# A decode block's weight and cache loads: one ring of 16 KiB slots on one queue, longer weight runs, accumulation by contraction chunk, and a last product in four column groups

## The chip, the cores and the metric

The kernel runs on one core of a Trainium2 chip. The metric is the device time of one execution in microseconds (us). Each kernel was timed in several rounds together with the kernel before on the same chip. The profile comes from one such execution; its span, from the first instruction to the last, is 1.7 to 2.0 us shorter than the reported time.

Engine names: PE is the TensorE's matmul side and PEld its weight loads; DVE is the VectorE, ACT the ScalarE, POOL the GpSimd, SP the SyncE. A "q" after the name means that engine's instruction queue, for example SPq, from which the loads are issued. HBM is the memory that holds the tensors, and SBUF the on-chip memory of 128 partitions in which loads land. L95 is line 95 of that kernel's source.

## The reference, cut to what matters

A decoder block for 4 sequences with one new token each: layer norm, attention over a cached window, and a gated feed-forward part. All tensors are bf16.

```python
# x (4,1,1024); k_cache, v_cache (4 batch, 4 kv heads, 8192, 128)
# wq (1024,4096)  wo (4096,1024)  w1, w3 (1024,3584)  w2 (3584,1024)
def _A_ref(x, k_cache, v_cache, wq, wo):
    W = min(4096, max(256, Sk // 4))            # 2048: the last 2048 keys
    q = (x @ wq).reshape(B, Sq, 32, 128).transpose(0, 2, 1, 3)
    k = jnp.repeat(k_cache[:, :, Sk - W:, :], 8, axis=1)
    v = jnp.repeat(v_cache[:, :, Sk - W:, :], 8, axis=1)
    p = softmax(einsum("bhqd,bhkd->bhqk", q, k) * 128 ** -0.5)
    return einsum("bhqk,bhkd->bhqd", p, v).transpose(...).reshape(B, Sq, 4096) @ wo
def _B_ref(x, w1, w3, w2):
    return (silu(x @ w1) * (x @ w3)) @ w2
h  = x + _A_ref(layernorm(x), k_cache, v_cache, wq, wo)
h2 = h + _B_ref(layernorm(h), w1, w3, w2)
```

With 4 rows of activations nearly every byte is used once: 55.6 MB of weights and cache must come from HBM (8.4 MB each for wq, K, V and wo; 7.3 MB each for w1, w3 and w2). The arithmetic is small.

## The kernel before

The parts that matter here, with cuts marked by "...". The SBUF tiles that receive the stream come from three pools. A padding tile in front of them moves their start to a multiple of 4096 bytes in each partition:

```python
    wq_v = A_wq.rearrange("(kc p) n -> p kc n", p=P)
    wo_v = A_wo.rearrange("(h p) n -> p h n", p=P)
    w1_v = B_w1.rearrange("(kc p) f -> p kc f", p=P)
    ...
    first_base = -(-nc.sbuf_base // 32) * 32
    pad_bytes = (-first_base) % 4096
    if pad_bytes:
        padpool = ctx.enter_context(tc.tile_pool(name="padpool", bufs=1))
        pad_t = padpool.tile([P, pad_bytes], mybir.dt.uint8)
    wpool = ctx.enter_context(tc.tile_pool(name="wpool", bufs=4))
    kpool = ctx.enter_context(tc.tile_pool(name="kpool", bufs=4))
    vpool = ctx.enter_context(tc.tile_pool(name="vpool", bufs=2))
```

Each load is one DMA of 2 MB. wq, w1 and w3 are read in blocks of 1024 output columns, so each contiguous piece (a "run") has 1024 x 2 bytes = 2 KiB; the last blocks of w1 and w3 have 512 columns, 1 KiB. K and V have runs of 4 KiB, wo and w2 of 2 KiB. V is issued from another queue (GpSimd).

```python
        dma.dma_start(out=wq_t[:], in_=wq_v[:, :, hb * HB * P : (hb + 1) * HB * P])     # dma = nc.sync
    ...
        nc.gpsimd.dma_start(out=vbig[:],
            in_=A_v_cache[b0, g0 : g0 + BGT, Sk - W : Sk, :].rearrange("g (p j) d -> p g j d", j=NK))
    ...
    FBLOCKS = [8, 8, 8, 4]
        dma.dma_start(out=w_t[:, :, : FB * P], in_=w_v[:, :, fc0_ * P : (fc0_ + FB) * P])
    ...
        dma.dma_start(out=w2_t[:, :FCB, :], in_=w2_v[:, fc0 : fc0 + FCB, :])
```

The last product uses 4 of the 128 output partitions, and its last load is 1 MB:

```python
    y2_ps = psB2.tile([B, D], FP32, tag="y2")
    ...
            for n in range(2):
                nc.tensor.matmul(y2_ps[:, n * 512 : (n + 1) * 512],
                    lhsT=hgT[:, fc, :], rhs=w2_t[:, fs, n * 512 : (n + 1) * 512],
                    start=(fc == 0), stop=(fc == FC - 1))
    res = act.tile([B, D], BF16)
    nc.vector.tensor_tensor(out=res[:], in0=y2_ps[:], in1=h1bd[:], op=ALU.add)
    dma.dma_start(out=out_flat, in_=res[:])
```

Of the kernel before, what the change touches and what calls it, by code (L numbers as in the profile page):

```python
# [10 lines left out]
P = 128  # L12
ACT = mybir.ActivationFunctionType
ALU = mybir.AluOpType
AX = mybir.AxisListType
BF16 = mybir.dt.bfloat16
FP32 = mybir.dt.float32

DEBUG = False
# [3 lines left out]
def kernel(  # L23
# [26 lines left out]
    assert Dh == P and W == NK * P and B * Hq == P  # L50
# [5 lines left out]
    wq_v = A_wq.rearrange("(kc p) n -> p kc n", p=P)  # L56
    wo_v = A_wo.rearrange("(h p) n -> p h n", p=P)
    w1_v = B_w1.rearrange("(kc p) f -> p kc f", p=P)
    w3_v = B_w3.rearrange("(kc p) f -> p kc f", p=P)
    w2_v = B_w2.rearrange("(fc p) n -> p fc n", p=P)  # L60

    dma = nc.sync

    if DEBUG:
        dbg_pool = ctx.enter_context(tc.tile_pool(name="dbg", bufs=1, space=bass.MemoryType.DRAM))

    def dump(name: str, ap: bass.AP):
        if not DEBUG:
            return
        t = dbg_pool.tile(list(ap.shape), ap.dtype, name=name, uniquify=False)  # L70
        nc.sync.dma_start(out=t[:], in_=ap)

    first_base = -(-nc.sbuf_base // 32) * 32
    pad_bytes = (-first_base) % 4096
    if pad_bytes:
        padpool = ctx.enter_context(tc.tile_pool(name="padpool", bufs=1))
        pad_t = padpool.tile([P, pad_bytes], mybir.dt.uint8)
    wpool = ctx.enter_context(tc.tile_pool(name="wpool", bufs=4))
    kpool = ctx.enter_context(tc.tile_pool(name="kpool", bufs=4))
    vpool = ctx.enter_context(tc.tile_pool(name="vpool", bufs=2))  # L80
# [3 lines left out]

    ident = const.tile([P, P], BF16)
    make_identity(nc, ident[:])
    eps_t = const.tile([P, 1], FP32)
    nc.vector.memset(eps_t[:], eps)

    WQB = 5  # L90
    HB = 8
    wq_tiles = []
    for hb in range(Hq // HB):
        wq_t = wpool.tile([P, KC, HB * P], BF16, tag="w16k")
        dma.dma_start(out=wq_t[:], in_=wq_v[:, :, hb * HB * P : (hb + 1) * HB * P])  # L95
        wq_tiles.append(wq_t)
        if hb == 0:
            x_sb = act.tile([B, D], BF16)
            dma.dma_start(out=x_sb[:], in_=x_flat)

    def layernorm_bf16(x_in_ap: bass.AP, tag: str) -> bass.AP:
        stats = act.tile([B, 2, nc.vector.BN_STATS_DIM], FP32, tag=tag + "_stats")
        for c in range(2):
            nc.vector.bn_stats(out=stats[:, c, :], in_=x_in_ap[:, c * 512 : (c + 1) * 512])
        mv = act.tile([B, nc.vector.BN_AGGR_DIM], FP32, tag=tag + "_mv")
        nc.vector.bn_aggr(out=mv[:], in_=stats[:])
        rstd = act.tile([B, 1], FP32, tag=tag + "_rstd")
        nc.scalar.activation(
            out=rstd[:], in_=mv[:, 1:2], func=ACT.Sqrt, bias=eps_t[:B], scale=1.0
        )  # L110
        nc.vector.reciprocal(out=rstd[:], in_=rstd[:])
        xn = act.tile([B, D], BF16, tag=tag + "_xn")
        nc.vector.tensor_scalar(  # L113
            out=xn[:],
            in0=x_in_ap,
            scalar1=mv[:, 0:1],
            scalar2=rstd[:, 0:1],
            op0=ALU.subtract,
            op1=ALU.mult,
        )  # L120
        return xn

    def transpose_bd_to_db(psum_pool, xn_ap: bass.AP, tag: str) -> bass.AP:
        tp_ps = psum_pool.tile([P, KC, B], BF16, tag="kt0")
        for kc in range(KC):
            nc.tensor.transpose(  # L126
                out=tp_ps[:, kc, :],
                in_=xn_ap[:, kc * P : (kc + 1) * P],
                identity=ident[:B, :B],
            )  # L130
        xT = act.tile([P, KC, B], BF16, tag=tag + "_xT")
        nc.vector.tensor_copy(out=xT[:], in_=tp_ps[:])
        return xT
# [3 lines left out]

    xn = layernorm_bf16(x_sb[:], "ln1")
    xnT = transpose_bd_to_db(psA, xn[:], "ln1")
    dump("dbg_xn", xn[:])  # L140
    dump("dbg_xnT", xnT[:])

    qT_ps = psA.tile([P, Hq, B], FP32, tag="kt1")
    for hb in range(Hq // HB):
        wq_t = wq_tiles[hb]
        for hh in range(HB):
            h = hb * HB + hh
            for kc in range(KC):
                nc.tensor.matmul(  # L149
                    qT_ps[:, h, :],  # L150
                    lhsT=wq_t[:, kc, hh * P : (hh + 1) * P],
                    rhs=xnT[:, kc, :],
                    start=(kc == 0),
                    stop=(kc == KC - 1),
                )

    Qm = act.tile([P, B * Hkv, P], BF16)
    nc.vector.memset(Qm[:], 0.0)
# [9 lines left out]
    dump("dbg_Qm", Qm[:])  # L168
# [3 lines left out]
    BGT = 4  # L172
    kbig_tiles = []
    for bt in range(B * Hkv // BGT):
        kbig = kpool.tile([P, BGT, NK, Dh], BF16, tag="kslot")
        b0, g0 = divmod(bt * BGT, Hkv)
        dma.dma_start(  # L177
            out=kbig[:],
            in_=A_k_cache[b0, g0 : g0 + BGT, Sk - W : Sk, :].rearrange("g (p j) d -> p g j d", j=NK),
        )  # L180
        kbig_tiles.append(kbig)
    for bg in range(B * Hkv):
        b, g = divmod(bg, Hkv)
        k_t = kbig_tiles[bg // BGT][:, bg % BGT]
        kT = ktpool.tile([P, NK, P], BF16, tag="kT")
        JPB = 4
        for jb in range(NK // JPB):
            kt_ps = psA.tile([P, JPB, P], FP32, tag=f"kt{jb % 4}")
            for jj in range(JPB):
                j = jb * JPB + jj  # L190
                nc.tensor.matmul(kt_ps[:, jj, :], lhsT=k_t[:, j, :], rhs=ident[:], start=True, stop=True)  # L191
            if jb % 2 == 0:
                nc.vector.tensor_copy(out=kT[:, jb * JPB : (jb + 1) * JPB, :], in_=kt_ps[:])  # L193
            else:
                nc.scalar.copy(out=kT[:, jb * JPB : (jb + 1) * JPB, :], in_=kt_ps[:])  # L195
        kT_tiles.append(kT)

        def emit_scores(bg2):
            for n in range(NSB):
                nc.tensor.matmul(  # L200
                    scores_ps[:, n * 512 : (n + 1) * 512],
                    lhsT=Qm[:, bg2, :],
                    rhs=kT_tiles[bg2][:, n * 4 : (n + 1) * 4, :],
                    start=(bg2 == 0),
                    stop=(bg2 == B * Hkv - 1),
                )

        if bg >= 1:
            emit_scores(bg - 1)
    emit_scores(B * Hkv - 1)  # L210

    v_tiles = []
    for bt in range(B * Hkv // BGT):
        b0, g0 = divmod(bt * BGT, Hkv)
        if bt < 2:
            vbig = vpool.tile([P, BGT, NK, Dh], BF16, tag="vslot")
        else:
            vbig = kpool.tile([P, BGT, NK, Dh], BF16, tag="kslot")
        nc.gpsimd.tensor_copy(out=vbig[0:1, 0, 0, 0:1], in_=Qm[0:1, 0, 0:1])
        nc.gpsimd.dma_start(  # L220
            out=vbig[:],
            in_=A_v_cache[b0, g0 : g0 + BGT, Sk - W : Sk, :].rearrange("g (p j) d -> p g j d", j=NK),
        )
        for gg in range(BGT):
            v_tiles.append(vbig[:, gg])
# [8 lines left out]
        out=Pm[:], in_=scores_ps[:], func=ACT.Exp, bias=nmax[:], scale=1.0,  # L234
        accum_out=rsum[:],
# [4 lines left out]
    nc.vector.tensor_scalar(  # L240
        out=Dm[:], in0=ident[:], scalar1=rinv[:, 0:1], scalar2=None, op0=ALU.mult
    )
    dump("dbg_Pm", Pm[:])
    dump("dbg_rsum", rsum[:])

    PT_sb = act.tile([P, NK, P], BF16)
    JB = 4
    for jb in range(NK // JB):
        pt_ps = psA.tile([P, JB, P], FP32, tag=f"kt{jb % 4}")
        for jj in range(JB):  # L250
            j = jb * JB + jj
            nc.tensor.matmul(  # L252
                pt_ps[:, jj, :],
                lhsT=Pm[:, j * P : (j + 1) * P],
                rhs=Dm[:],
                start=True,
                stop=True,
            )
        nc.vector.tensor_copy(out=PT_sb[:, jb * JB : (jb + 1) * JB, :], in_=pt_ps[:])  # L259
    dump("dbg_PT", PT_sb[:])  # L260

    OT_ps = psA.tile([P, B, Hq], FP32, tag="kt1")
    for bg in range(B * Hkv):
        b, g = divmod(bg, Hkv)
        v_t = v_tiles[bg]
        for j in range(NK):
            nc.tensor.matmul(  # L267
                OT_ps[:, b, g * REP : (g + 1) * REP],
                lhsT=v_t[:, j, :],
# [3 lines left out]
            )  # L273
    OT_sb = act.tile([P, Hq, B], BF16)
    nc.vector.tensor_copy(out=OT_sb[:].rearrange("p h b -> p b h"), in_=OT_ps[:])
    dump("dbg_OT", OT_sb[:])
    psA_cm.__exit__(None, None, None)

    psB_cm = tc.tile_pool(name="psB", bufs=1, space=bass.MemoryType.PSUM)
    psB = psB_cm.__enter__()  # L280
    xT = transpose_bd_to_db(psB, x_sb[:], "x")
    dump("dbg_hnT0", xT[:])
    yT_ps = psB.tile([P, KC, B], FP32, tag="yt")
    HB2 = 8
    wo_tiles = []
    for hb in range(Hq // HB2):
        wo_t = wpool.tile([P, HB2, D], BF16, tag="w16k")
# [154 lines left out]
```

## Time and profile before

| | before |
|---|---|
| time, median of 4 runs (lowest to highest) | 149.81 us (149.66 to 151.16) |
| span of the profile | 147.8 us |
| PE busy, DVE busy | 59%, 25% |
| moved by DMA | 55.8 MB in 24,542 packets |

Three lines of the profile's page cut the span into 40 equal slices of 3.7 us. DMA is the busy share of the 16 DMA engines in tenths (9 is 90% or more), GB/s what they moved, and the third line sums the packets. One data packet is one contiguous run; the packet records of the trace have 17,928 of 2 KiB, 4,096 of 4 KiB and 2,048 of 1 KiB, and the 456 packets under 512 B are records of 4 bytes.

```profile
DMA  4999999999999999999999999999999999999600
GB/s 96 408 410 409 406 406 423 422 413 421 422 419 419 420 421 412 419 414 408 409 406 407 405 411 402 404 409 404 408 405 408 386 387 401 409 410 408 247 6 2
DMA packets 24542, 55.81 MB, mean 378 GB/s; under 512 B 456, under 2 KB 2504, under 8 KB 24528
```

The DMA engines are full from the second slice to the 37th, while no other engine is full throughout. So the kernel is bound by its stream of loads, and only two things count: how fast the stream runs, and what comes after its end. The windows view gives the rate in chosen stretches. Its columns are the stretch in us and its length, then busy us (and instructions) of PE, PEld, DVE, ACT and POOL, then the clock that the TensorE was granted (1.00 is full), the busy share of the DMA engines, and GB/s:

```profile
3.00:20.00 17.00, 4.08 (x136) 3.93 (x136) 2.33 (x6) 0.29 (x1) 0.00 (x0) 1.00 1.05 405
30.00:60.00 30.00, 26.16 (x263) 19.21 (x264) 17.04 (x26) 14.25 (x26) 1.84 (x4) 0.94 1.03 419
68.00:82.00 14.00, 8.79 (x266) 8.54 (x267) 3.32 (x8) 4.62 (x4) 0.00 (x0) 0.51 1.05 408
100.00:114.00 14.00, 8.75 (x306) 8.37 (x305) 1.49 (x3) 0.00 (x0) 0.00 (x0) 0.50 1.05 407
115.00:122.00 7.00, 2.88 (x96) 2.71 (x96) 0.00 (x0) 0.44 (x1) 0.00 (x0) 0.50 1.08 388
...
137.00:138.00 1.00, 0.71 (x4) 0.17 (x2) 0.00 (x0) 0.00 (x0) 0.00 (x0) 1.00 0.98 377
138.00:139.00 1.00, 0.45 (x3) 0.18 (x3) 0.00 (x0) 0.00 (x0) 0.00 (x0) 1.00 0.59 219
...
140.00:141.00 1.00, 1.00 (x7) 0.42 (x5) 0.00 (x0) 0.00 (x0) 0.00 (x0) 1.00 0.21 80
141.00:142.00 1.00, 1.00 (x6) 0.35 (x5) 0.00 (x0) 0.00 (x0) 0.00 (x0) 1.00 0.00 0
```

The rate follows the run length: 405 to 408 GB/s for 2 KiB runs (wq at 3 to 20 us, wo at 68, w1/w3 at 100), 419 for 4 KiB (K and V at 30 to 60), 388 for 1 KiB (at 115). After 137 us the rate decays: some of the 16 engines are done, others are not, and the last is done at 141. The chain of waits (start, length, what the end of the kernel waited for) ends so:

```profile
138.55 5.35 PE y_ps L401 x24
...
143.93 1.21 DVE res L410
```

A landing at 138.55 releases 24 matmuls of the last product, 5.35 us, then the add on 4 partitions, 1.21 us, and then the output DMA. From the last landing of the stream (141.2, by the trace's records) to the end (147.8) there are 6.6 us.

### The profile page before, as it was taken

Reading aid. Unit: us, or ns where it says so; the run is one execution under the profiler, and the core shown is the slowest. Engines: PE = TensorE matmul, PEld = TensorE weight load, DVE = VectorE, ACT = ScalarE, POOL = GpSimd, SP = SyncE. Lnnn points to the kernel's source line nnn. Section 1 sums busy time; section 2 is a strip of 40 time slices with the busy share of each in tenths; the row PEclk is TensorE's granted clock in tenths of the full one; section 3 lists DMA queues with packets and bytes.
Section 4 is the critical chain, followed back from the end, with each engine's and each line's share of the span. In section 5 each row is a group of like instructions: output and inputs, shape, how many; then the busy total and the mean of one; then the engine's idle time right before and its main releaser. Section 6 shows DMA issues by size and latency. Waiting matters only on the chain.

```text
span 147.8 us, 3563 instructions
## 1 busy us (share of the span) xinstructions
PE 87.2 (59%) x1648; PEld 65.9 (45%) x1648; DVE 37.0 (25%) x84; ACT 25.5 (17%) x41; POOL 4.4 (3%) x14
## 2 busy tenths in 40 slices
PE   0008252289992996980389494464695162299790
PEld 0008142286771774740379394443685152033230
DVE  3050000355772375755340100024000004000002
ACT  3000000044562354634700000000000013000000
POOL 1000000500202000000000000000000000000000
PEclk9999999999999599997555555555555555559998
DMA  4999999999999999999999999999999999999600
GB/s 96 408 410 409 406 406 423 422 413 421 422 419 419 420 421 412 419 414 408 409 406 407 405 411 402 404 409 404 408 405 408 386 387 401 409 410 408 247 6 2
DMA packets 24542, 55.81 MB, mean 378 GB/s; under 512 B 456, under 2 KB 2504, under 8 KB 24528
## 3 DMA queue, kind: packets, MB, share of 16 engines
q1 hardware_dynamic: 22416, 47.20, 82.3%
q0 software_dynamic: 2112, 8.39, 13.8%
q8 instruction: 13, 0.21, 0.5%
q14 instruction: 1, 0.01, 0.0%
HBM read 55.58 MB, written 0.01 MB: 376 GB/s over the span
## 4 chain that ended last, share of the span: by engine, by line
DMA 50%; SPq 25%; PE 15%; DVE 4%; ACT 2%; issue 1%; ACTq 0%
DMA kbig<-in_A_k_cache_dram 24%; DMA big<-in_B_w_dram 13%; DMA w_t<-in_B_w_dram 12%; SPq L177 7%; SPq L314 7%; SPq L95 6%; PE OT_ps L267 5%; SPq L323 4%; PE y_ps L401 4%; PE scores_ps L200 3%; PE kt_ps L191 3%; DVE PT_sb L259 2%; DVE rmax L228 2%; ACT Pm L233 1%; PE uT_ps L367 1%
## 5 line engine op out<-in xcount | busy, mean ns | idle before, releaser
L193 DVE CAST kT<-kt_ps 128x512 bf16<-128x512 f32 x32 | 20.9, 687 | 15.8 <-PE kt_ps L191 5.6
L195 ACT CAST kT<-kt_ps 128x512 bf16<-128x512 f32 x32 | 17.5, 588 | 37.0 <-PE kt_ps L191 24.2
L191 PE MATMUL kt_ps<-ident,kbig 128*128 128x128 bf16 x256 | 19.2, 237 | 6.9 <-DMA kbig<-in_A_k_cache_dram 6.9
L191 PEld LDWEIGHTS <-kbig 128*128 128x128 bf16 x256 | 17.6, 107 | 11.0 <-DMA kbig<-in_A_k_cache_dram 8.1
L367 PEld LDWEIGHTS <-big 128*128 128x128 bf16 x448 | 12.5, 104 | 12.0 <-DMA big<-in_B_w_dram 11.7
L401 PE MATMUL y_ps<-w_t,hgT 128*4 128x512 bf16 x56 | 14.8, 429 | 5.0 <-DMA w_t<-in_B_w_dram 5.0
L200 PE MATMUL scores_ps<-kT,Qm 128*128 128x512 bf16 x64 | 17.4, 399 | 0.0
L149 PE MATMUL qT_ps<-xT,wq_t 128*128 128x4 bf16 x256 | 7.4, 166 | 7.9 <-DMA wq_t<-in_A_wq_dram 7.6
L401 PEld LDWEIGHTS <-hgT 128*4 128x4 bf16 x56 | 5.2, 93 | 14.1 <-issue 7.7
L149 PEld LDWEIGHTS <-wq_t 128*128 128x128 bf16 x256 | 7.2, 104 | 8.2 <-DMA wq_t<-in_A_wq_dram 7.8
L367 PE MATMUL uT_ps<-hnT,big 128*128 128x4 bf16 x224 | 6.6, 166 | 6.5 <-DMA big<-in_B_w_dram 6.3
L293 PE MATMUL yT_ps<-OT_sb,wo_t 128*128 128x4 bf16 x256 | 7.5, 166 | 4.4 <-issue 4.4
L293 PEld LDWEIGHTS <-wo_t 128*128 128x128 bf16 x256 | 7.1, 104 | 4.7 <-issue 4.6
L367 PE MATMUL gT_ps<-hnT,big 128*128 128x4 bf16 x224 | 6.5, 166 | 4.5 <-DMA big<-in_B_w_dram 4.5
L200 PEld LDWEIGHTS <-Qm 128*128 128x128 bf16 x64 | 6.0, 104 | 4.5 <-issue 1.0
L267 PE MATMUL OT_ps<-PT_sb,vbig 128*128 128x8 bf16 x256 | 7.2, 168 | 0.7 <-DVE PT_sb L259 0.6
L267 PEld LDWEIGHTS <-vbig 128*128 128x128 bf16 x256 | 7.2, 104 | 1.0 <-issue 1.0
L126 PE MATMUL tp_ps<-ident,xn 4*128 4x4 bf16 x8 | 0.4, 164 | 11.2 <-DVE xn L113 11.2
L410 DVE TENSOR_TENSOR res<-y_ps,h1bd 4x1024 bf16<-4x1024 f32 x1 | 1.2, 1212 | 18.9 <-PE y_ps L401 18.9
L252 PE MATMUL pt_ps<-Dm,Pm 128*128 128x128 bf16 x16 | 1.9, 311 | 6.6 <-DVE Dm L240 6.6
L378 DVE TENSOR_SCALAR eg<-eg 128x112 f32<-128x112 f32 x1 | 0.2, 219 | 21.4 <-ACT eg L377 21.4
L126 PEld LDWEIGHTS <-xn 4*128 4x128 bf16 x8 | 0.3, 100 | 11.2 <-DVE xn L113 11.2
(56 smaller groups left out, 34.7 us busy)
## 6 DMA issues: line engine op xcount, KB each, us to landing
big<-in_B_w_dram SPq DMA_DIRECT2D x6, 2048.0 KB, 19.8
wq_t<-in_A_wq_dram SPq DMA_DIRECT2D x4, 2048.0 KB, 14.9
kbig<-in_A_k_cache_dram SPq DMA_DIRECT2D x4, 2048.0 KB, 25.6
wo_t<-in_A_wo_dram SPq DMA_DIRECT2D x4, 2048.0 KB, 25.7
vbig<-in_A_v_cache_dram POOLq DMA_DIRECT2D x4, 2048.0 KB, 24.0
w_t<-in_B_w_dram SPq DMA_DIRECT2D x3, 2048.0 KB, 15.5
big<-in_B_w_dram SPq DMA_DIRECT2D x2, 1024.0 KB, 15.0
w_t<-in_B_w_dram SPq DMA_DIRECT2D x1, 1024.0 KB, 16.4
```

Of the source, the lines that this page charges most:

```text
L95: dma.dma_start(out=wq_t[:], in_=wq_v[:, :, hb * HB * P : (hb + 1) * HB * P])
L149: nc.tensor.matmul(qT_ps[:, h, :], lhsT=wq_t[:, kc, hh * P : (hh + 1) * P], rhs=xnT[:, kc, :], start=(kc == 0), stop=(kc == KC - 1),)
L177: dma.dma_start(out=kbig[:], in_=A_k_cache[b0, g0 : g0 + BGT, Sk - W : Sk, :].rearrange("g (p j) d -> p g j d", j=NK),)
L191: nc.tensor.matmul(kt_ps[:, jj, :], lhsT=k_t[:, j, :], rhs=ident[:], start=True, stop=True)
L193: nc.vector.tensor_copy(out=kT[:, jb * JPB : (jb + 1) * JPB, :], in_=kt_ps[:])
L195: nc.scalar.copy(out=kT[:, jb * JPB : (jb + 1) * JPB, :], in_=kt_ps[:])
L200: nc.tensor.matmul(scores_ps[:, n * 512 : (n + 1) * 512], lhsT=Qm[:, bg2, :], rhs=kT_tiles[bg2][:, n * 4 : (n + 1) * 4, :], start=(bg2 == ...
L267: nc.tensor.matmul(OT_ps[:, b, g * REP : (g + 1) * REP], lhsT=v_t[:, j, :], rhs=PT_sb[:, j, b * Hq + g * REP : b * Hq + (g + 1) * REP], st ...
L293: nc.tensor.matmul(yT_ps[:, dc, :], lhsT=wo_tiles[hb][:, hh, dc * P : (dc + 1) * P], rhs=OT_sb[:, h, :], start=(h == 0), stop=(h == Hq - 1),)
L314: dma.dma_start(out=w_t[:, :, : FB * P], in_=w_v[:, :, fc0_ * P : (fc0_ + FB) * P])
L367: nc.tensor.matmul(out_ps[:, fc, :], lhsT=w_t[:, kc, fs * P : (fs + 1) * P], rhs=hnT[:, kc, :], start=(kc == 0), stop=(kc == KC - 1),)
L401: nc.tensor.matmul(y2_ps[:, n * 512 : (n + 1) * 512], lhsT=hgT[:, fc, :], rhs=w2_t[:, fs, n * 512 : (n + 1) * 512], start=(fc == 0), stop= ...
```

## The change

Its intent is to make the stream faster and its tail shorter. All loads go through one ring of ten 16 KiB slots (2 MB over 128 partitions) on one queue, in a fixed order, each issued as soon as its slot is free. Weights are read as whole rows, so that runs get longer: 16 KiB for wq (two rows), 7 KiB for w1 and w3, 8 KiB for most of w2. For that, the products accumulate chunk by chunk of the contraction. The last product is spread over four groups of matmuls, called column groups here: each takes 256 of the 1024 output columns and writes to output partitions of its own (from 0, 32, 64 and 96). And the last load is cut to one row of 256 KB.

```diff
-    wq_v = A_wq.rearrange("(kc p) n -> p kc n", p=P)
...
-    first_base = -(-nc.sbuf_base // 32) * 32
-    pad_bytes = (-first_base) % 4096
-    if pad_bytes:
-        padpool = ctx.enter_context(tc.tile_pool(name="padpool", bufs=1))
-        pad_t = padpool.tile([P, pad_bytes], mybir.dt.uint8)
-    wpool = ctx.enter_context(tc.tile_pool(name="wpool", bufs=4))
-    kpool = ctx.enter_context(tc.tile_pool(name="kpool", bufs=4))
-    vpool = ctx.enter_context(tc.tile_pool(name="vpool", bufs=2))
+    stream = ctx.enter_context(tc.tile_pool(name="stream", bufs=10))
...
+    wq_v = A_wq.rearrange("(p kc) n -> p kc n", kc=KC)
+    wo_v = A_wo.rearrange("(h p) n -> p h n", p=P)
+    w13_v = [w.rearrange("(kc p) f -> p kc f", p=P) for w in (B_w1, B_w3)]
+    w2_v = B_w2.rearrange("(fb p r) n -> p fb r n", p=P, r=RPC)
+    def load_wq(c):
+        wq_t = stream.tile([P, KPC, Hq * Dh], BF16, tag="s")
+        nc.sync.dma_start(out=wq_t[:], in_=wq_v[:, c * KPC : (c + 1) * KPC, :])
...
+    def load_w13(i, c):
+        w13_t = stream.tile([P, KPC, F], BF16, tag="s")
+        nc.sync.dma_start(out=w13_t[:], in_=w13_v[i][:, c * KPC : (c + 1) * KPC, :])
...
+    plan = (
+        [("wq", load_wq, (c,)) for c in range(KC // KPC)]
+        + [("k", load_kv, (A_k_cache, b)) for b in range(B)]
+        + [("v", load_kv, (A_v_cache, b)) for b in range(B)]
+        + [("wo", load_wo, (c,)) for c in range(Hq // HPC)]
+        + [("w1", load_w13, (0, c)) for c in range(KC // KPC)]
+        + [("w3", load_w13, (1, c)) for c in range(KC // KPC)]
+        + [("w2", load_w2, (c, [RPC] if c < NW2 - 1 else [2, 1, 1])) for c in range(NW2)]
+    )
...
+    for i in range(2):
+        for kc in range(KC):
+            w_t = loaded[("w1", "w3")[i]][kc // KPC]
+            w_v = w_t[:, kc % KPC, :].rearrange("k (fb p r) -> k fb r p", p=P, r=RPC)
+            for fc in range(FC):
+                nc.tensor.matmul(gu_ps[i][:, fc, :],
+                    lhsT=w_v[:, fc // RPC, fc % RPC, :], rhs=hnT[:, kc, :], ...)
...
-            for n in range(2):
-                nc.tensor.matmul(
-                    y2_ps[:, n * 512 : (n + 1) * 512],
+        for j in range(JG):
+            nc.tensor.matmul(
+                y2_ps[32 * j : 32 * j + B, :],
+                lhsT=hgT[:, fc, :],
+                rhs=w2_t[:, fc % RPC, j * CG : (j + 1) * CG],
...
+    res = act.tile([P, CG], BF16)
+    nc.vector.tensor_copy(out=res[:], in_=y2_ps[:])
+    for j in range(JG):
+        q = nc.sync if j % 2 == 0 else nc.scalar
+        q.dma_start(out=out_flat[:, j * CG : (j + 1) * CG], in_=res[32 * j : 32 * j + B, :])
```

Counted from the shapes, the data packets fall from 24,064 to 11,904: wq 512, K and V 4096, wo 4096, w1 and w3 2048, w2 1152.

## The prediction

> What bounds it now. The DMA stream. The page's slice row shows the DMA engines nine tenths busy or more from the second slice to the 37th; the TensorE is busy 59%. The chain of waits is half DMA and a quarter the load queue, and ends in a tail that the stream does not cover. By the windows view the stream starts at about 2.8 us, holds full rate to 137.5 and thins out until 141, some of the 16 engines finishing late. In the last product a landing releases the TensorE at 138.55; 24 matmuls take 5.35 us, the add on 4 partitions 1.21, the output 2.7 more to the end at 147.8. The reported time is 1.9 us above this span.
>
> What the stream costs. Slice rates by run length: 2 KiB runs (weights) 406 to 410 GB/s, 4 KiB (K, V) about 420, the 1 KiB loads about 387. My estimate from these: 4.9 ns a packet per engine plus bytes at 435 GB/s. [...] Before: about 24,000 packets, 7.4 us of packet cost in about 135 us. After: wq in 8 to 16 KiB runs, w1 and w3 in 7, w2 mostly 8; K, V (4) and wo (2) unchanged: about 12,000 packets, 3.7 us. Gain 3.7 us, all critical if the stream never stalls.
>
> Does it stall? Ten slots of 2 MB give about 49 us of lookahead. K will land by about 43 us (57.8 now, as V shares the engines from 27.7); the K stage, 1.75 us a head in the chain, ends at about 56 instead of 66, the V product at 73, before wo has landed (83). I expect no slot wait to reach the DMA engines. The 448 gate and up matmuls pass at 28 ns each (128 in 3.57 us): 1.6 us a chunk against 4.3 of loading.
>
> The tail. w2 is consumed as it lands; the last load is one row (256 KB), so 4 matmuls of 256 columns follow it, not 24 of 512. [...] Even serial, at about 110 ns with the clock up (222 for 512 columns in the chain), 112 of them fit in 17 us of stream. Estimate from last landing: matmuls 0.5 us, copy of 128x256 0.4 (0.69 for 128x512 here), output 2.7 to 3.1: 4 in all, against 6.6 from the last byte now. Gain 2.6 us. The engines' scatter (slowest about 2.4 us past the mean) should stay.
>
> Sum: 6.3 us less: span about 141.5, time about 143.4.
>
> What would show it. Over 425 GB/s while wq, w1, w3, w2 load, 420 for K and V, 408 for wo; DMA full until about 136; near 12,000 packets; under 5 us after the last landing; K stage over before 60.
>
> What would make it wrong. (1) Long runs no faster than 4 KiB, or the wq reads (64 KiB apart between partitions) slower: 3 us less gain. (2) The w1/w3 weight reads, at a step of four elements, which nothing here shows: if a load takes its recorded 104 ns unoverlapped, 448 take 47 us, the TensorE becomes the limit, and no gain. (3) Column groups serial at the low clock (0.5), 213 ns each. (4) A slot freed late.

The rule of 4.9 ns a packet and 435 GB/s is an estimate from the three slice rates: it gives 385, 408 and 421 GB/s for runs of 1, 2 and 4 KiB, where 387, 406 to 410 and 420 were read (a straight line through the packet times at 387, 408 and 420 GB/s gives 4.5 ns and 432 GB/s). The 213 ns of risk (3) is half of the 0.43 us at which the matmuls of 512 columns follow each other in the kernel before at a granted clock of 0.50 (weight loads at 128.68, 129.11, ... 132.95 us).

## The result, and the profile after

The changed kernel takes 145.87 us (145.76 to 145.96, 4 runs). A ratio here is the mean time of one kernel's fast runs over that of the other's of the same rounds, so it is not quite the ratio of the medians quoted. It is 0.9715, with a 95% interval of 0.9669 to 0.9761: faster, by 3.9 us where 6.4 were forecast.

The page's lines after (slices of 3.6 us):

```profile
DMA  5999999999999999999999999999999999999930
GB/s 166 418 437 437 432 432 381 406 408 413 408 407 410 409 407 406 413 395 387 385 388 381 388 407 408 422 418 422 410 424 412 418 424 420 416 425 412 404 133 5
DMA packets 12487, 55.82 MB, mean 387 GB/s; under 512 B 548, under 2 KB 564, under 8 KB 11192
```

The packets halved as counted, and the engines stay full to the end of the stream without a hole: no wait for a slot reached them. The windows view of the same stages, wq, K and V, wo, w1/w3, and the end:

```profile
3.00:20.00 17.00, 5.38 (x173) 5.14 (x174) 2.24 (x8) 0.29 (x1) 0.00 (x0) 1.00 1.01 427
22.00:40.00 18.00, 12.45 (x176) 10.48 (x179) 8.53 (x28) 6.00 (x11) 0.00 (x0) 1.00 1.02 410
...
65.00:82.00 17.00, 12.31 (x381) 11.84 (x382) 3.62 (x8) 1.49 (x3) 0.00 (x0) 0.50 1.05 386
88.00:114.00 26.00, 12.86 (x331) 11.33 (x328) 2.74 (x13) 1.84 (x3) 0.00 (x0) 0.50 1.01 417
...
137.00:138.00 1.00, 0.04 (x4) 0.04 (x7) 0.00 (x0) 0.00 (x0) 0.00 (x0) 0.50 0.55 219
138.00:139.00 1.00, 0.98 (x16) 0.47 (x16) 0.00 (x0) 0.00 (x0) 0.00 (x0) 0.50 0.37 147
139.00:140.00 1.00, 0.77 (x12) 0.32 (x12) 0.00 (x0) 0.00 (x0) 0.00 (x0) 0.50 0.27 102
140.00:141.00 1.00, 0.59 (x8) 0.09 (x3) 0.10 (x1) 0.00 (x0) 0.00 (x0) 0.50 0.00 0
```

wq with its long runs went from 405 to 427 GB/s. But K and V, whose runs were not touched, fell from 419 to 410, and wo, also not touched, from 408 to 386. w1/w3 came to 417 in 7 KiB runs where the forecast rule gives 427. So the last byte came at about 140 us, only 1 us earlier than before, where the forecast had 3.7. The end of the chain after:

```profile
125.49 14.93 DMA w_t<-in_B_w_dram
...
140.46 0.41 PE y_ps L365 x4
...
140.90 0.42 DVE res L375
```

Four matmuls and the copy follow the last landing at 140.46. From there to the end at 144.1 there are 3.6 us. So the tail gave what it was to give. Two groups of instructions (line, engine, operation, tiles, shape, count, then busy us and mean ns of one, then idle us before them and what ended it) answer the two worries about the TensorE. First the weight loads and the last product of the kernel before:

```profile
L401 PE MATMUL y_ps<-w_t,hgT 128*4 128x512 bf16 x56 | 14.8, 429 | 5.0 <-DMA w_t<-in_B_w_dram 5.0
L367 PEld LDWEIGHTS <-big 128*128 128x128 bf16 x448 | 12.5, 104 | 12.0 <-DMA big<-in_B_w_dram 11.7 <-issue 0.3
```

The same work in the changed kernel:

```profile
L341 PEld LDWEIGHTS <-w_t 128*128 128x128 bf16 x448 | 15.6, 118 | 16.5 <-DMA w_t<-in_B_w_dram 15.7 <-issue 0.8
...
L365 PE MATMUL y_ps<-w_t,hgT 128*4 128x256 bf16 x112 | 7.5, 404 | 8.3 <-DMA w_t<-in_B_w_dram 8.2
```

The 448 gate and up weight loads, which now pick every fourth column, took 15.6 us in place of 12.5: 35 ns each in place of 28, slower but far from the 35 us of stream that they have (14.7 MB at 417 GB/s). The last product is busy 7.5 us in place of 14.8. One row of the timeline after (start, length, what, idle before it) shows the column groups at work:

```profile
128.00 1.02 PE L365 MATMUL y_ps<-w_t,hgT 128*4 128x256 bf16 x16 [1.47 <-DMA w_t<-in_B_w_dram]
```

16 matmuls of 256 columns pass in 1.02 us, 64 ns each, at a granted clock of 0.50.

### The profile page after: what moved, and what is told of

It is laid out like the page before. It is cut to its first block, busy times and chain, and to the rows that moved or that the text cites. A ratio compares the mean times of both kernels' runs of the same rounds, so it can differ in the third digit from the quotient of the medians.

```text
span 144.1 us, 3687 instructions
## 1 busy us (share of the span) xinstructions
PE 80.7 (56%) x1707; PEld 66.3 (46%) x1712; DVE 35.3 (25%) x84; ACT 25.4 (18%) x41; POOL 0.7 (0%) x6
## 2 busy tenths in 40 slices
DMA packets 12487, 55.82 MB, mean 387 GB/s; under 512 B 548, under 2 KB 564, under 8 KB 11192
## 4 chain that ended last, share of the span: by engine, by line
DMA 62%; PE 25%; DVE 3%; ACT 3%; issue 3%; SPq 2%; ACTq 0%
DMA w_t<-in_B_w_dram 30%; DMA kv_t<-in_A_k_cache_dram 18%; DMA wo_t<-in_A_wo_dram 14%; PE kt_ps L214 11%; PE scores_ps L197 9%; DVE rmax L228 2%; ACT Pm L233 1%; PE yT_ps L280 1%; PE gT_ps L341 1%; SPq L70 1%; SPq L87 1%; ACT L233 1%; PE pt_ps L246 0%; PE y_ps L323 0%; PE sums_ps L301 0%
## 5 line engine op out<-in xcount | busy, mean ns | idle before, releaser
L341 PEld LDWEIGHTS <-w_t 128*128 128x128 bf16 x448 | 15.6, 118 | 16.5 <-DMA w_t<-in_B_w_dram 15.7
L214 PE MATMUL kt_ps<-ident,kv_t 128*128 128x128 bf16 x256 | 18.4, 231 | 3.2 <-DMA kv_t<-in_A_k_cache_dram 3.2
L214 PEld LDWEIGHTS <-kv_t 128*128 128x128 bf16 x256 | 17.0, 104 | 6.6 <-DMA kv_t<-in_A_k_cache_dram 3.3
L197 PE MATMUL scores_ps<-kT,Qm 128*128 128x512 bf16 x59 | 15.2, 379 | 0.3
L170 PE MATMUL qT_ps<-xnT,wq_t 128*128 128x4 bf16 x256 | 7.5, 166 | 12.5 <-DMA wq_t<-in_A_wq_dram 12.5
L341 PE MATMUL uT_ps<-hnT,w_t 128*128 128x4 bf16 x224 | 8.1, 173 | 9.4 <-DMA w_t<-in_B_w_dram 9.4
L365 PE MATMUL y_ps<-w_t,hgT 128*4 128x256 bf16 x112 | 7.5, 404 | 8.3 <-DMA w_t<-in_B_w_dram 8.2
L341 PE MATMUL gT_ps<-hnT,w_t 128*128 128x4 bf16 x224 | 8.1, 173 | 6.1 <-DMA w_t<-in_B_w_dram 5.7
L257 PE MATMUL OT_ps<-PT_sb,kv_t 128*128 128x8 bf16 x256 | 7.6, 168 | 3.3 <-issue 2.6
L365 PEld LDWEIGHTS <-hgT 128*4 128x4 bf16 x112 | 3.5, 104 | 12.1 <-issue 10.2
L257 PEld LDWEIGHTS <-kv_t 128*128 128x128 bf16 x256 | 7.3, 104 | 3.8 <-issue 3.7
## 6 DMA issues: line engine op xcount, KB each, us to landing
w_t<-in_B_w_dram SPq DMA_DIRECT2D x6, 1024.0 KB, 25.9
```

What stands on the lines that cost most here:

```text
L170: nc.tensor.matmul(qT_ps[:, h, :], lhsT=wq_t[:, kc % KPC, h * P : (h + 1) * P], rhs=xnT[:, kc, :], start=(kc == 0 and h == 0), stop=(kc == ...
L197: nc.tensor.matmul(scores_ps[:, n * 512 : (n + 1) * 512], lhsT=Qm[:, bg2, :], rhs=kT_tiles[bg2][:, n * 4 : (n + 1) * 4, :], start=(bg2 == ...
L214: nc.tensor.matmul(kt_ps[:, jj, :], lhsT=k_t[:, g, j, :], rhs=ident[:], start=True, stop=True)
L257: nc.tensor.matmul(OT_ps[:, b, g * REP : (g + 1) * REP], lhsT=v_t[:, g, j, :], rhs=PT_sb[:, j, b * Hq + g * REP : b * Hq + (g + 1) * REP], ...
L341: nc.tensor.matmul(gu_ps[i][:, fc, :], lhsT=w_v[:, fc // RPC, fc % RPC, :], rhs=hnT[:, kc, :], start=(kc == 0 and fc == 0), stop=(kc == KC ...
L365: nc.tensor.matmul(y2_ps[32 * j : 32 * j + B, :], lhsT=hgT[:, fc, :], rhs=w2_t[:, fc % RPC, j * CG : (j + 1) * CG], start=False, stop=(fc ...
```

## The experiments

The question: why did loads that the change left alone become slower? Theory A: the dropped padding. The ring's slots no longer start on a boundary that the DMA engines like, and each packet pays for it. Rival B: the single queue with ten loads outstanding. The old kernel had V on a second queue and fewer loads waiting. The 4.5 to 6.5 ns of theory A in experiment 1 are an estimate; by the rates that it names a packet differs by 4.6 ns at 4 KiB, 4.4 at 2 KiB and 5.8 at 7 KiB, on each of 16 engines. The record marks every run as correct; the last leaves out work on purpose, and only its time is read. The edits of experiments 3 to 6 are shown against the padding lines of experiment 1 or 3; experiments 7 to 12 carry the 128 bytes of padding of experiment 3, which their edits here leave out. Experiments 1 to 4 ran together on one chip (kernel before: 150.03 us), 5 to 8 together (before: 150.00), 9 to 12 together (before: 150.77). The kernel before was 0.7 us slower in the third group; the aligned kernel does not show it (the last landing is at 137.29 us in experiment 3 and at 137.32 in experiment 11). Where kernels of different groups are compared below, differences under about 0.5 us are not read.

### 1. The padding put back

```diff
+    first_base = -(-nc.sbuf_base // 32) * 32
+    pad_bytes = (-first_base) % 4096
+    padpool = ctx.enter_context(tc.tile_pool(name="padpool", bufs=1))
+    pad_t = padpool.tile([P, pad_bytes], mybir.dt.uint8)
     stream = ctx.enter_context(tc.tile_pool(name="stream", bufs=10))
```

> The changed kernel with the old kernel's padding put back, so that the ring starts on a multiple of 4096 bytes in each partition instead of 128 bytes past a multiple of 256. Theory A (misaligned destinations cost some 4.5 to 6.5 ns a packet): K and V load at about 420 GB/s again (408 without), wo at about 406 (385), w1/w3 near 427 (418); 12,000 packets, so 3 to 3.5 us less: about 142.5 us. Rival B (one queue, ten loads deep, slows the engines; the old kernel had V on a second queue): rates and time as without the padding, 145.9 us.

Measured: 142.76 us, ratio to before 0.9517 (0.9496 to 0.9539). The windows view of this run in K and V, wo, and w1/w3:

```profile
22.00:40.00 18.00, 12.94 (x179) 10.66 (x180) 8.83 (x28) 6.29 (x12) 0.00 (x0) 1.00 1.02 419
62.00:80.00 18.00, 11.29 (x348) 10.88 (x349) 3.62 (x8) 4.17 (x4) 0.00 (x0) 0.54 1.05 407
88.00:114.00 26.00, 14.25 (x369) 12.80 (x369) 2.73 (x13) 1.84 (x3) 0.00 (x0) 0.50 1.01 424
```

K and V are back at 419 GB/s and wo at 407, on one queue with the ring ten deep. Theory A holds; rival B cannot explain it, since nothing that B speaks of was altered.

### 2. The old kernel without its padding

```diff
-    pad_bytes = (-first_base) % 4096
+    pad_bytes = 0
```

> The kernel before with its padding set to nothing and no other edit. Theory A: its 24,000 packets pay 4.5 ns each over 16 engines, 6 to 7 us more: about 156 us, with 2 KiB-run loads at about 385 GB/s. Rival B: 149.8 us, rates of 406 to 420 GB/s as before.

Measured: 156.16 us, ratio 1.0406 (1.0381 to 1.043). The windows view in wq and in wo, both 2 KiB runs:

```profile
5.00:18.00 13.00, 4.08 (x136) 3.93 (x136) 2.33 (x6) 0.29 (x1) 0.00 (x0) 1.00 1.05 389
...
75.00:88.00 13.00, 9.84 (x296) 9.45 (x295) 3.10 (x6) 0.53 (x1) 0.00 (x0) 0.50 1.05 387
```

The same loads that ran at 405 to 408 GB/s run at 387 to 389. The loss is 6.1 us over 24,064 packets. Spread over 16 engines, this is 6.1 x 16 / 24,064 = 4.1 ns a packet. The changed kernel loses 145.87 - 142.76 = 3.1 us over 11,904 packets, 4.2 ns each. About one number covers both kernels.

### 3 and 4. How much alignment is needed

```diff
-    pad_bytes = (-first_base) % 4096
+    pad_bytes = (-first_base) % 256        # experiment 3;  % 512 in experiment 4
```

> The changed kernel with 128 bytes of padding: the ring starts on a multiple of 256 bytes but not of 512. If theory A holds and 256-byte alignment is what counts: as with the 4096-byte padding, about 142.5 us. If a coarser one counts: as without padding, 145.9 us. Rival B: 145.9 us.

> The changed kernel with 384 bytes of padding: the ring starts on a multiple of 512 but not of 1024 bytes. Theory A with an alignment of 256 or 512 bytes: about 142.5 us. With a page of 4096 bytes: 145.9 us. Rival B: 145.9 us.

Measured: 142.78 us (0.952) and 142.83 us (0.9522). A multiple of 256 bytes is enough; 512 or 4096 add nothing. The padding needed is 128 bytes.

### 5 and 6. Does the cost depend on how far off the start is?

Experiments 1 to 4 do not show what a packet off the multiple pays for. Theory A1 is a guess: it pays for the bytes between the 256-byte multiple below its start and the start. Then the 4.1 to 4.2 ns measured at 128 bytes would halve at 64 bytes and grow by half at 192.

```diff
-    pad_bytes = (-first_base) % 256
+    pad_bytes = (-first_base) % 256 + 64   # experiment 5;  + 192 in experiment 6
```

> The ring starts 64 bytes past a multiple of 256 (aligned: 142.8 us; 128 bytes past, as in the changed kernel: 145.9). Theory A1: a misaligned packet pays for the bytes between the 256-byte boundary below it and its start, so half of the cost at 128 bytes: about 144.3 us. Theory A2: any start off the boundary costs the same: about 145.9 us. Theory A3: 64-byte alignment is enough: 142.8 us.

> The ring starts 192 bytes past a multiple of 256. Theory A1 (cost grows with the distance from the boundary below): one and a half times the cost at 128 bytes, about 147.4 us. Theory A2 (the same cost wherever it starts): about 145.9 us. If the cost goes by the largest power of two that divides the start, it equals the 64-byte case.

Measured: 146.14 us (0.9743) at 64 bytes past the boundary and 146.01 us (0.9735) at 192, against 145.87 at 128 (0.9715). The cost is the same at all three, so theory A2 holds and the reading by unused bytes (A1) falls. The packet records in the traces show the cost directly, by the mean time of one packet: 84.6 ns for 2 KiB, 159.5 for 4 KiB, 273.0 for 7 KiB and 310.3 for 8 KiB in experiment 3, and 88.8, 163.5, 277.1 and 314.6 in the changed kernel; experiments 5 and 6 are within 0.5 ns of the latter. So the time is lost in the packets themselves, about 4 ns each whatever their size from 2 to 8 KiB (the 512 packets of 16 KiB show no rise: 632 ns in both). What costs a packet this constant time, no run shows.

### 7. The old run lengths in the aligned kernel (confounded)

```diff
-        nc.sync.dma_start(out=wq_t[:], in_=wq_v[:, c * KPC : (c + 1) * KPC, :])
+        for n in range(0, Hq * Dh, 1024):
+            nc.sync.dma_start(out=wq_t[:, :, n : n + 1024], in_=wq_v[:, c * KPC : (c + 1) * KPC, n : n + 1024])
     # w1 and w3 likewise, in pieces of 1024, 1024, 1024 and 512 columns; w2 one row at a time
-        + [("w2", load_w2, (c, [RPC] if c < NW2 - 1 else [2, 1, 1])) for c in range(NW2)]
+        + [("w2", load_w2, (c, [1, 1, 1, 1])) for c in range(NW2)]
```

> The changed kernel, aligned to 256 bytes, with its weights loaded in the run lengths of the kernel before: wq and w2 in 2 KiB runs, w1 and w3 in 2 KiB and 1 KiB runs; about 24,000 packets in place of 12,500, and 45 loads more. If a packet costs 4.9 ns per engine: 3.6 us more[...]: about 146.6 us, w1/w3 at about 405 GB/s. If run length did not matter and the gain of the aligned kernel lay in the tail: 142.8 us.

Measured: 150.57 us (149.09 to 150.8; ratio 1.0018, 0.9964 to 1.0071), 4 us more than the first theory said and 8 more than the second. The profile is of the fastest of its runs, 149.09 us. By the pages, this run has 880 more records under 512 B than the changed kernel, 16 for each of 55 loads; at 9 ns, which is what a record of 4 bytes takes in the changed kernel's trace, they are 0.5 us on 16 engines (an estimate). The experiment changed two things: run lengths, and the number of loads (88 in place of 33; the expectation miscounted this as 45 more, it is 55). The windows view in w1/w3 and in w2:

```profile
88.00:114.00 26.00, 16.48 (x408) 14.24 (x405) 2.73 (x13) 1.84 (x3) 0.00 (x0) 0.50 1.06 401
120.00:138.00 18.00, 10.26 (x158) 4.75 (x156) 0.27 (x1) 0.00 (x0) 0.00 (x0) 0.50 0.98 341
```

w1/w3 ran at 401 GB/s in place of 423, as short runs should. But w2, in loads of 256 KB, ran at 341, below any run-length effect seen. The load queue's own waits (line, what it waited for, us in total, times, longest) show more waiting there:

```profile
SPq L94 <- DMA w_t<-in_B_w_dram: 15.5, 23, 1.2
...
SPq L101 <- DMA w_t<-in_B_w_dram: 12.1, 26, 1.0
```

The queue waits for its own earlier loads to land, 49 times, 27.6 us in all, before it issues the next ones; in experiment 3 it does so 5 times, 13.0 us in all. The profile gives 5.7 us from issue to landing for the 256 KB loads here and 25.9 us for the 1 MB loads of the changed kernel, so little is queued ahead. That this is what slows w2 is not shown: the engines' busy share is still 0.98 there, and by the packet records a twentieth of the 2 KiB packets last from about 100 ns to over 300, the others 84. How many loads may be under way, and what sets it, no run here settles.

### 8. The last load whole

```diff
-        + [("w2", load_w2, (c, [RPC] if c < NW2 - 1 else [2, 1, 1])) for c in range(NW2)]
+        + [("w2", load_w2, (c, [RPC])) for c in range(NW2)]
```

> The changed kernel, aligned to 256 bytes, with the last load of w2 whole (1 MB) and not cut in two rows, one and one. 16 matmuls in place of 4 follow the last landing, 1.0 us in place of 0.4 by the trace: about 0.6 us more, 143.4 us. If the matmuls did not overlap: 3 us more.

Measured: 143.59 us (0.957, 0.9542 to 0.9597) against 142.78 for experiment 3 in the earlier rounds: 0.8 us, about as expected. The chain shows 16 matmuls in 1.05 us after a landing at 137.36, where experiment 3 has 4 in 0.41 after one at 137.29.

### 9. One run length alone

This is experiment 7 done more cleanly: only w1 and w3 land in shorter runs, in loads that stay large, though there are 8 more of them.

```diff
-        w13_t = stream.tile([P, KPC, F], BF16, tag="s")
-        nc.sync.dma_start(out=w13_t[:], in_=w13_v[i][:, c * KPC : (c + 1) * KPC, :])
+        w13_t = stream.tile([P, F // 512, KPC, 512], BF16, tag="s")
+        for k in range(KPC):
+            nc.sync.dma_start(
+                out=w13_t[:, :, k, :], in_=w13_v[i][:, c * KPC + k, :].rearrange("p (fb x) -> p fb x", x=512)
+            )
...
-            w_v = w_t[:, kc % KPC, :].rearrange("k (fb p r) -> k fb r p", p=P, r=RPC)
+            w_v = w_t[:, :, kc % KPC, :].rearrange("k fb (p r) -> k fb r p", p=P, r=RPC)
```

> The changed kernel, aligned to 256 bytes, with w1 and w3 landing in 1 KiB runs in place of 7 KiB (the tile's layout is reordered; 16 loads of 0.9 MB in place of 8 of 1.8). 12,288 more packets. If each costs 4.9 ns on its engine: 3.8 us more, 146.5 us, and w1/w3 at about 387 GB/s in place of 424. If a run's length does not count and the excess of the short-run kernel before this (150.6 us) came from its many small loads alone: 142.8 us.

Measured: 146.50 us (0.9712, 0.9682 to 0.9743). The windows view in w1/w3, of experiment 3 and then of this run:

```profile
88.00:114.00 26.00, 14.24 (x369) 12.80 (x369) 2.74 (x13) 1.84 (x3) 0.00 (x0) 0.50 1.01 423
88.00:114.00 26.00, 13.06 (x317) 11.37 (x317) 2.74 (x13) 1.85 (x3) 0.00 (x0) 0.50 1.08 382
```

382 GB/s in place of 423, and 3.7 us more than experiment 3 (spans 144.6 and 140.9, so 3.7 by the spans too). The two runs are of different groups, but the stages that the edit left alone ran at the same rates in both (419 to 420 GB/s in K and V, 407 in wo), and 14.7 MB at 382 in place of 423 GB/s are 3.7 us by themselves. 3.7 x 16 / 12,288 = 4.8 ns a packet: the prediction's figure, measured by itself.

### 10. The last product in one column group

```diff
-    y2_ps = psB.tile([P, CG], FP32, tag="y2")
-    nc.vector.memset(y2_ps[:], 0.0)
+    y2_ps = psB.tile([B, D], FP32, tag="y2")
...
-        for j in range(JG):
+        for j in range(2):
             nc.tensor.matmul(
-                y2_ps[32 * j : 32 * j + B, :],
+                y2_ps[:, j * 512 : (j + 1) * 512],
                 lhsT=hgT[:, fc, :],
-                rhs=w2_t[:, fc % RPC, j * CG : (j + 1) * CG],
+                rhs=w2_t[:, fc % RPC, j * 512 : (j + 1) * 512],
...
-    res = act.tile([P, CG], BF16)
+    res = act.tile([B, D], BF16)
```

> The changed kernel, aligned to 256 bytes, with the last product as the kernel before has it: 2 matmuls of 512 columns for a row block, on 4 partitions, a copy of 4x1024, one output load. If the four column groups matter: the TensorE falls behind w2 at the low clock (0.43 us a matmul against 2.45 us of stream for 8 of them), and the copy takes 1.2 us in place of 0.42; 1.5 to 2.5 us more, about 144.8 us. If they do not (the stream still ends last and only the copy counts): under 1 us more.

Measured: 144.09 us (0.9554, 0.9529 to 0.9579), 1.3 us more than experiment 3: between the two expectations. The timeline of this run:

```profile
122.54 11.67 PE L368 MATMUL y_ps<-w_t,hgT 128*4 128x512 bf16 x40 [0.40 <-DMA w_t<-in_B_w_dram]
...
134.81 3.61 PE L368 MATMUL y_ps<-w_t,hgT 128*4 128x512 bf16 x16 [0.61 <-DMA w_t<-in_B_w_dram]
...
138.46 1.21 DVE L378 CAST res<-y_ps 4x1024 bf16<-4x1024 f32 x1 [16.02 <-PE y_ps L368]
```

The TensorE works without a pause from 122.5 to 134.2 on 40 matmuls, catches up with the stream, waits 0.6 us, and ends 16 more at 138.42; experiment 3 is done with its matmuls at 137.70. That is 0.7 us, and the copy on 4 partitions adds 0.8; the single output load gives back 0.25 (from the end of the copy to the end of the span 2.5 us, 2.8 in experiment 3). In the first 5.5 us the weight loads of these matmuls start every 0.43 us, at a granted clock of 0.50; the clock is 1.00 from 128 us on, and 512 columns then take 0.22 us. So the falling behind is real, and the rising clock repairs most of it: by an estimate from these figures, 56 matmuls at 0.43 us each would have ended at about 146.6 us.

### 11. V on a second queue

```diff
-        nc.sync.dma_start(
+        q = nc.sync if cache is A_k_cache else nc.gpsimd
+        q.dma_start(
             out=kv_t[:], in_=cache[b, :, Sk - W : Sk, :].rearrange("g (p j) d -> p g j d", j=NK)
```

> The changed kernel, aligned to 256 bytes, with the V loads on a second queue (issued from GpSimd), so that V shares the engines with wq and K from the start and K lands later. Theory (the stream alone counts, the order of landing does not): the K stage ends some 8 to 10 us later, and the time stays at 142.8 us within 0.5. Rival (the single queue is part of the gain): 1 us or more longer.

Measured: 143.10 us (0.9491, 0.9465 to 0.9516). The scores end and the row maximum starts at 73.5 us, against 59.3 in the changed kernel: 14 us later, where 8 to 10 were expected. The line of the row maximum in the tile view (duration, first and last start), changed kernel and then this run:

```profile
L228 DVE TENSOR_REDUCE rmax<-scores_ps x1: 2292/2292/2292, 59.3 to 59.3; 128x1 f32<-128x2048 f32 x1
L233 DVE TENSOR_REDUCE rmax<-scores_ps x1: 2292/2292/2292, 73.5 to 73.5; 128x1 f32<-128x2048 f32 x1
```

The time moved by 0.3 us. The order of landing in the first half of the kernel, and the single queue as such, are worth nothing here that these runs resolve.

### 12. Fewer instructions (wrong result)

The profile's page lists a queue of kind "instruction": 13 packets, 0.21 MB, which it counts as 0.5 or 0.6% of the time of the same 16 DMA engines.

```diff
-        for h in range(Hq):
+        for h in range(Hq) if kc % KPC == 0 else []:      # q: half of the matmuls
...
-        for j in range(NK):
+        for j in range(0, NK, 4):                         # V: a quarter
...
-        for dc in range(KC):
+        for dc in range(KC) if h % 4 == 0 else []:        # wo: a quarter
...
-            for fc in range(FC):
+            for fc in range(FC) if kc % KPC == 0 else []: # gate and up: half
```

> Wrong result on purpose: the changed kernel, aligned to 256 bytes, with 736 of its matmuls left out (half of the q, gate and up products, three quarters of the V and wo products); all loads stay. Theory: the engines that finish late, 136.99 in place of about 134, are those that also fetched 16 KiB blocks of instructions, about 1 us each, 13 in all. With 7 or 8 blocks the scatter at the end shrinks from about 3.4 us to about 2, and the time falls by 0.5 to 1.5 us, to about 141.8. Rival (some engines are slower on their own, or lag for the data's sake): scatter and time stay, 142.8 us.

Measured: 141.36 us (0.9372, 0.9347 to 0.9397), 1.4 us less than experiment 3. The page's line for the instruction queue of experiment 3 (packets, MB, share of the engines):

```profile
q8 instruction: 13, 0.21, 0.5%
```

The windows view of experiment 3 at the end of its stream:

```profile
133.00:134.00 1.00, 0.43 (x8) 0.13 (x1) 0.00 (x0) 0.00 (x0) 0.00 (x0) 0.50 1.02 410
134.00:135.00 1.00, 0.15 (x4) 0.10 (x7) 0.00 (x0) 0.00 (x0) 0.00 (x0) 0.50 0.56 223
135.00:136.00 1.00, 0.88 (x16) 0.40 (x9) 0.00 (x0) 0.00 (x0) 0.00 (x0) 0.50 0.39 154
136.00:137.00 1.00, 0.92 (x12) 0.32 (x12) 0.00 (x0) 0.00 (x0) 0.00 (x0) 0.50 0.28 109
```

The same line of the page of this run:

```profile
q8 instruction: 7, 0.11, 0.3%
```

The windows view of this run at the end of its stream:

```profile
133.00:134.00 1.00, 0.64 (x16) 0.43 (x16) 0.00 (x0) 0.00 (x0) 0.00 (x0) 0.50 1.02 404
134.00:135.00 1.00, 0.74 (x16) 0.31 (x9) 0.00 (x0) 0.00 (x0) 0.00 (x0) 0.50 0.52 199
135.00:136.00 1.00, 0.73 (x16) 0.18 (x7) 0.00 (x0) 0.00 (x0) 0.00 (x0) 0.50 0.18 68
136.00:137.00 1.00, 0.27 (x4) 0.00 (x0) 0.42 (x1) 0.00 (x0) 0.00 (x0) 0.50 0.00 0
```

Both streams run at full rate until 134 us. With 13 instruction packets, a quarter of the engines are still busy at 136 to 137; with 7, none. By the packet records an instruction packet of 16 KiB lasts 0.92 us in the kernel before and 1.06 us in the changed kernel, each the mean of 13. The records do not name the engine of a packet, so which engines fetched is not seen. So most of the late finish went with the instruction fetches. The run also did less matmul work, which the explanation does not need, but which the run does not exclude either.

## Why the prediction was right or wrong

Right in direction, too hopeful by 2.5 us. Point by point:

- **Bound by the stream: right.** DMA is full in the page's slices before and after, and in experiment 11 a 14 us delay of the scores moved the time by 0.3 us.
- **Run length: right, with the right size.** The rule "4.9 ns a packet" was read from three rates of the old trace; experiment 9 measured 4.8. The packet count (12,487 on the page) and the 3.7 us that follow from it came once the ring was aligned: experiments 1, 3 and 4 are 7.2 to 7.3 us faster than before on their chip. Of this, about (24,064 - 11,904) x 4.8 / 16 = 3.6 us is packets and 6.6 - 3.6 = 3.0 us the tail. The rest, 0.6 us, is about what an earlier start is worth, which the prediction did not count: in the first 4 us the aligned kernel moved 0.79 MB and the kernel before 0.48, a lead of 0.7 to 0.8 us at 405 to 428 GB/s (an estimate). One rate fell short: w1 and w3 ran at 423 to 424 GB/s even when aligned, where over 425 was forecast.
- **"K, V (4) and wo (2) unchanged": this step failed.** Their run lengths were unchanged, their destinations were not. The term of the sum that was mis-sized is the cost of a packet: 4.9 ns was read from a kernel whose slots start on 4096-byte multiples, and was applied to a ring that starts 128 bytes off a 256-byte boundary. There a packet costs 4.1 to 4.2 ns more, by the times and by the packet records. Over 11,904 packets that is 3.1 us, more than the whole miss of 2.5. The diff showed the padding going away; the prediction read past it.
- **Supply of slots: right.** No hole in the DMA row; the K stage ended at 59.3 (forecast 56, "before 60"). The V product ended at 78.6, not 73, which did not reach the stream.
- **Tail: right.** Forecast 4 us after the last landing, measured 3.6; matmuls 0.41 (0.5 forecast), copy 0.42 (0.4). Experiments 8 and 10 give the shares: cutting the last load 0.8 us, column groups and narrow copy 1.3.
- **Scatter of the engines "should stay": right,** and in experiment 12, which also did less matmul work, most of it went with the instruction fetches.
- **The named risks.** (1) wq's reads were not slow: 427 GB/s. (2) Strided weight loads cost 35 ns in place of 28, no limit. No experiment undid the step of four alone, but wq's loads in the changed kernel, in the same chunk order at a step of one, took 28 ns (7.1 us for 256, at a granted clock of 1.00), and so did wo's at 0.50 (7.2 us for 256). (3) The column groups did overlap: 64 ns a matmul of 256 columns at clock 0.50, where experiment 10 has 430 ns for 512, so by estimate 215 for 256; a factor of 3.4. (4) No slot was late. The risk that struck was not on the list.

The version to keep is the changed kernel with 128 bytes of padding (experiment 3): 142.78 us, 0.952 of before, and faster than both kernels.

## What to carry to other kernels

When a kernel is bound by its loads, count packets and see where each one starts: in this case a packet cost 4.8 ns beyond its bytes, and 4.1 more when its SBUF destination was not on a 256-byte multiple, so a 128-byte padding tile was worth as much as most of the rewrite of the weight layout. When a rewrite makes something slower that it did not mean to touch, compare that stage's rate before and after, and look through the diff for the removed lines that seem to do nothing. Lengthen runs by layout: here runs of 1 KiB moved 382 to 388 GB/s, 2 KiB 405 to 408, 4 KiB 419, 7 KiB 423 and 16 KiB 428 (the last two in experiment 3), all on aligned slots. Do not cut loads into small ones: w2 in loads of 256 KB and runs of 2 KiB ran at 341 GB/s in experiment 7, for a cause that is not shown. And keep the last load and the work after it small: the cut of the last load was worth 0.8 us here, and the column groups with the narrow copy 1.3.
